# A float64 guard by absolute value and maximum, and a feed-forward half scaled by two instructions over two planes

## The chip, the core and the metric

The kernel runs on one core of a Trainium2 chip. The metric is the time of one execution on the device in microseconds (us). Five engines work side by side, each through its own queue in the order of the program: TensorE (PE, with its weight loads PEld), VectorE (DVE), ScalarE (ACT), GpSimd (POOL) and SyncE (SP), which only issues DMAs. They wait for one another through semaphores.

## The reference

Three stages follow one another: attention with a decay (4 batches, 8 heads, 576 positions, head width 64), a feed-forward network over the 2304 tokens of width 512, and a mixture of eight experts of which each token takes one. What matters here is the middle stage:

```python
h = x @ w_in                                   # x: 2304 x 512, w_in: 512 x 2048
g = np.where(h >= 1, h, np.where(h <= -1, 0.0, (h + 1) ** 2 / 4.0))
x = (g @ w_out).astype(np.float32)             # w_out: 2048 x 512
...
w_in = np.random.randn(d_model, d_ff).astype(np.float32) * (1.0 / np.sqrt(d_model))    # float64
w_out = np.random.randn(d_ff, d_model).astype(np.float32) * (1.0 / np.sqrt(d_ff))      # float64
```

The factor is a NumPy float64 scalar, and so the two weights come as float64, eight bytes an element, and the kernel turns them into float32 itself. They are read as pairs of 32-bit words: the high word holds the sign, the exponent and the upper bits of the mantissa.

## The kernel before

**Order.** A planner in the kernel (class `Order`) runs all stages as Python generators. Each `yield dve(...)`, `act(...)`, `pool2(...)`, `dma(...)` or `Use("PE", ...)` asks for an engine for so many planned nanoseconds with a priority (a smaller number goes first), and the step after it is asked for when the planned time and a latency are over. The order in which requests are granted is the order of each engine's queue; the chip then runs the queues with the real durations. A changed planned duration therefore moves instructions everywhere. `dve(n, fn, prio, fast)` plans 144 + 1.05 n ns, or 144 + 0.6 n with `fast`.

**Attention** (lines 505 to 735) takes pairs of heads: scores (line 505, tile SR), softmax on DVE, ACT and POOL (583 to 593), transposes (607), weighted sums (650, 669, 726). Raw inputs come by SP's DMAs (373), are transposed and split into a high and a low part, and are laid out in tiles `stk`, four parts each, by DMAs from `stk` to `stk` (438 to 449). The last of these for a tile, line 438, is a copy asked for at low priority.

**The feed-forward network** is done in two halves of the hidden width. `half0` (names with p) takes nine blocks of 256 tokens: block n makes hidden units in pairs (line 910, tile `hp`, two banks), `ffn_hidden` works each out (ACT 922, DVE 926 and 927, ACT 931, POOL 932), and line 1038 adds each into `accp`, a tile of four planes of 256 columns in two PSUM banks, of which there is one buffer. When all eight pieces of a block are added, `ffn_finish0` scales the four planes by 4 into a tile `x2_0` (lines 1064 on ACT and 1065 on DVE) and gives the buffer back; only then can block n + 1 add its first piece. Most of `half0` is fitted into attention; the last blocks run alone. `half1` (names with r) follows with 512 tokens at a time, then the experts (names with m). `half1` first loads its input (SP, line 891, tiles `rx`), and splits it (ACT 895, DVE 896), asked for when the last hidden unit of `half0` has been issued.

**The weights** are turned by `float64_piece`, 16 pieces of 128x512 for each half: the first 16 (tiles `wa`, raw words `war`, work tile `wax`) during attention, the other 16 (`wb`, `wbr`, `wbx`) during the last blocks of `half0`. A piece is a chain over one work tile: ACT squares the high words (853), DVE zeroes those whose square is under a bound (854), shifts and masks (856), brings back sign and top exponent bit (858), adds bits of the low word (860), ACT rounds to the high part (864), POOL subtracts for the low part (865). The work tile has one buffer, so that the next piece starts when POOL is done.

Of the kernel before, what the change touches and what calls it, by code (L numbers as in the profile page):

```python
# [13 lines left out]
AF = mybir.ActivationFunctionType  # L14
ALU = mybir.AluOpType
# [6 lines left out]
MIN64 = 2.0 ** -15 * 1.125  # L22


def f32(ap):
    return ap.bitcast(F32)
# [49 lines left out]
class Order:  # L76
# [90 lines left out]
    def done(self, ev):  # L167
        ev.n -= 1
        if ev.n == 0:
            for g in ev.waiters:  # L170
                self.at(self.now, lambda g=g: self.step(g, None))
            ev.waiters = []
# [18 lines left out]
def dve(n, fn, prio=5.0, fast=False):  # L191
    return Use("DVE", 144 + n * (0.6 if fast else 1.05), fn, prio)


def act(n, fn, prio=5.0, more=0.0):
    return Use("ACT", 155 + n / 1.2 + more, fn, prio)
# [6 lines left out]
def pool2(n, fn, prio=5.0):  # L203
    return Use("POOL", 180 + 2.3 * n, fn, prio)
# [19 lines left out]
def kernel(  # L224
# [14 lines left out]
    nc = tc.nc  # L239
    B, H, S, D = q.shape  # L240
    NT, DM = out.shape
# [5 lines left out]
    TB = 256  # L247
# [22 lines left out]
    late = {}  # L270
# [570 lines left out]
    def float64_piece(g, src, hi, lo, ok, name, prio):  # L841
        def put():
            r = fp.tile([P, DM], I64, tag="wraw", name=name + "r", bufs=2)
            nc.sync.dma_start(r.rearrange("p (c f) -> p c f", c=src.shape[1]), src)
            return r
        r = yield dma(P * DM * 8, put, 3)
        gx = yield (wx_b, 1)
        w = r.bitcast(I32).rearrange("p (n w) -> p n w", w=2)
        lw, hw = w[:, :, 0], w[:, :, 1]


        x = fp.tile([P, DM], I32, tag="wx", name=name + "x", bufs=1)
        yield act(DM, lambda: nc.scalar.activation(f32(x), f32(hw), AF.Square), prio)
        yield dve(DM, lambda: nc.vector.scalar_tensor_tensor(
            f32(hw), f32(x), MIN64 * MIN64, f32(hw), ALU.is_ge, ALU.mult), prio)
        yield dve(DM, lambda: nc.vector.tensor_scalar(
            x, hw, 3, 0x3FFFFFFF, ALU.logical_shift_left, ALU.bitwise_and), prio, True)
        yield dve(DM, lambda: nc.vector.scalar_tensor_tensor(
            x, hw, -0x40000000, x, ALU.bitwise_and, ALU.bitwise_or), prio)
        yield dve(DM, lambda: nc.vector.scalar_tensor_tensor(  # L860
            x, lw, 29, x, ALU.logical_shift_right, ALU.bitwise_or), prio)
        give(wr_b, g)
        xv = f32(x).rearrange("p (c f) -> p c f", c=src.shape[1])
        yield act(DM, lambda: nc.scalar.copy(hi, xv), prio)
        yield pool2(DM, lambda: nc.gpsimd.tensor_tensor(lo, xv, f32(hi), ALU.subtract), prio)
        give(wx_b, gx)
        done(ok)
# [78 lines left out]
    class Layer:  # L946
# [51 lines left out]
        def run2(self):  # L998
            for n in self.blocks:
                W, w = self.weights(), self.widths[n]  # L1000
                ga = yield (acc_b, 1)
                acc = None
                for u in self.units[n]:
                    yield self.g_ok[n, u]
                    GH, GL, gg = self.G.pop((n, u))
                    for k, s in enumerate(u):
                        yield W.ok[1][s]
                        if acc is None:
                            acc = psf.tile([P, 4, TB], F32, tag="acc", name=f"acc{self.name}{n}",
                                           bufs=1)  # L1010
                            if self is half0:
                                acc = [acc[:, d] for d in range(KC)]
                            else:
                                acc = [a[:, d] for a in (
                                    acc.rearrange("p (a d) t -> p a (d t)", a=2),
                                    late["psg"].tile([P, 2, 2 * TB], F32, tag="accB",
                                                     name=f"accB{self.name}{n}")) for d in range(2)]
                        gh, gl = (g[:, w * k:w * k + w] for g in (GH, GL))
                        yield Use("PE", mm(w, 3 * KC),
                                  lambda: self.second(acc, s, W, gh, gl), self.prio + 0.5,  # L1020
                                  after=0.0 if s < NF - 1 else None)
                    give(g_b, gg)
                yield from self.finish(n, acc)
                give(acc_b, ga)
            done(self.all_done)
# [34 lines left out]
    def ffn_finish0(n, acc):  # L1060
        g = yield (x2_b, 1)
        r = block("x2", g, f"x2_0_{n}")
        for d in (0, 2):
            yield act(TB, lambda: nc.scalar.mul(r[:, d], acc[d], 4.0), 0)
            yield dve(TB, lambda: nc.vector.tensor_scalar(r[:, d + 1], acc[d + 1], 4.0, None,  # L1065
                                                          ALU.mult), 0)
        go(keep(x2p[n], r, x2p_ok[n], g))

# [574 lines left out]
```

## Time and profile before

| | us |
|---|---|
| median of 3 runs (lowest, highest) | 919.18 (918.75, 919.71) |
| the profiled execution, its own time | 919.89 |
| its span, first to last instruction | 918.1 |
| TensorE busy in the span | 881.1 (96%) |
| VectorE busy | 519.9 (57%) |
| ScalarE busy | 408.7 (45%) |
| GpSimd busy | 328.5 (36%) |

Busy shares are means over stages. What counts for the time is where TensorE stands idle, for what it waits there, and the clock that it is granted (1.00 is full speed).

### The profile page before, as it was taken

How to read it: one execution, taken by the hardware profiler on the slowest of the kernel's cores; microseconds unless marked ns; L12 is line 12 of the kernel's file. 1: busy time of each engine (PE TensorE's matmuls, PEld its weight loads, DVE VectorE, ACT ScalarE, POOL GpSimd, SP SyncE). 2: the span in 40 equal slices, each digit the busy share in tenths (PEclk: the TensorE clock that was granted, in tenths of full speed). 3: DMA queues.
4: the chain of work that ended last, by engine and by line, in shares of the span. 5: the costliest groups of instructions: out<-in, count | busy, mean ns of one | idle time of the engine just before them, and what ended most of it. 6: DMA issues, size and time to landing. Idle time of an engine off the chain costs nothing. (4 is left out here: it accounts for less than half of the span.)

```text
span 918.1 us, 15151 instructions
## 1 busy us (share of the span) xinstructions
PE 881.1 (96%) x5224; PEld 752.6 (82%) x5224; DVE 519.9 (57%) x1323; ACT 408.7 (45%) x931; POOL 328.5 (36%) x342
## 2 busy tenths in 40 slices
PE   8999889999999999999799999999999999999995
PEld 6456668989998999999788888888998888888884
DVE  4878588678788747677763454376543512122331
ACT  3668677677777745443443243323333212111220
POOL 4567578565566624344342123222210132000000
PEclk9999899999999999999899999999999999999998
DMA  6669888676776407333421134744330203403220
GB/s 131 144 139 216 183 188 164 143 142 146 169 149 127 107 27 143 119 121 104 161 92 46 58 122 120 225 165 140 124 127 24 91 2 100 175 24 115 69 92 24
DMA packets 156165, 109.23 MB, mean 119 GB/s; under 512 B 103652, under 2 KB 126692, under 8 KB 156080
## 3 DMA queue, kind: packets, MB, share of 16 engines
q1 hardware_dynamic: 153080, 104.04, 43.4%
q0 software_dynamic: 3008, 4.22, 1.8%
q8 instruction: 42, 0.69, 0.3%
q14 instruction: 35, 0.29, 0.1%
HBM read 67.23 MB, written 24.75 MB: 100 GB/s over the span
## 5 line engine op out<-in xcount | busy, mean ns | idle before, releaser
L593 POOL TENSOR_SCALAR P<-P,st 128x512 f32<-128x512 f32 (+2 forms) x144 | 96.4, 676 | 108.9 <-DVE st L592 49.4
L932 POOL TENSOR_TENSOR glr<-gr,ghr 128x512 fp32r<-128x512 f32 x36 | 47.6, 1321 | 146.0 <-PE accBr L1038 100.0
L587 ACT ACTIVATE P<-P,st 128x512 f32<-128x512 f32 (+2 forms) x144 | 84.1, 585 | 34.1 <-DVE st L583 30.7
L505 PE MATMUL SR<-stk 128*128 128x256 f32 (+5 forms) x356 | 85.2, 351 | 7.7 <-DVE st L583 4.4
L910 PE MATMUL hr<-rx,wb 128*128 128x512 f32 (+1 forms) x384 | 89.0, 365 | 0.0
L1038 PE MATMUL accp<-ghp,wa 128*128 128x256 f32 x576 | 83.9, 289 | 5.2 <-DVE x L1065 5.2
L910 PE MATMUL hm<-mx,wm 128*128 128x512 f32 (+1 forms) x336 | 87.7, 381 | 0.0
L941 DVE SCALAR_TENSOR_TENSOR glm<-hm,ghm 128x512 fp32r<-128x512 f32 x36 | 24.8, 690 | 100.3 <-PE accBm L1046 75.9
L940 ACT ACTIVATE ghm<-hm 128x512 fp32r<-128x512 f32 x36 | 21.5, 598 | 132.5 <-PE accBm L1046 119.5
L1038 PEld LDWEIGHTS accp<-ghp,wa 128*128 128x128 f32 x576 | 75.5, 194 | 6.1 <-DVE x L1065 5.8
L910 PEld LDWEIGHTS hr<-rx,wb 128*128 128x128 f32 x384 | 65.7, 189 | 12.1
L583 DVE CUSTOM_DVE_ANT_0 P<-SR,masks 128x512 f32<-128x512 f32 (+1 forms) x112 | 53.6, 485 | 36.5 <-PE SR L505 30.4
L505 PEld LDWEIGHTS SR<-stk 128*128 128x128 f32 (+1 forms) x356 | 53.4, 183 | 24.6 <-issue 8.4
L932 POOL TENSOR_TENSOR glp<-gp,ghp 128x512 fp32r<-128x512 f32 x36 | 49.0, 1361 | 64.7 <-ACT ghp L931 46.8
L910 PEld LDWEIGHTS hm<-mx,wm 128*128 128x128 f32 x336 | 60.7, 188 | 12.6 <-DVE glm L941 0.3
L607 PE MATMUL T<-ident,P 128*128 128x128 f32 x384 | 64.0, 279 | 4.0 <-POOL P L593 3.0
L922 ACT ACTIVATE tr<-hr,quarter 128x512 f32<-128x512 f32 x36 | 24.7, 687 | 65.6 <-DVE gr L927 49.4
L607 PEld LDWEIGHTS T<-ident,P 128*128 128x128 f32 x384 | 43.7, 141 | 11.3 <-POOL P L593 6.7
L926 DVE SCALAR_TENSOR_TENSOR gr<-tr 128x512 f32<-128x512 f32 x36 | 24.8, 689 | 44.2 <-POOL glr L932 42.6
L1046 PE MATMUL accm<-wm,ghm 128*128 128x512 f32 x160 | 49.0, 395 | 0.0
L1038 PE MATMUL accr<-ghr,wb 128*128 128x512 f32 (+1 forms) x160 | 47.1, 376 | 0.0
L1466 POOL DMA_INDIRECT table<-ent,posi x18 | 17.8, 991 | 80.5 <-DVE ent L1455 52.0
(308 smaller groups left out, 2034.0 us busy)
## 6 DMA issues: line engine op xcount, KB each, us to landing
stk<-stk SPq DMA_DIRECT2D x26, 288.0 KB
stk<-stk SPq DMA_DIRECT2D x13, 432.0 KB
rawq<-in_q_dram SPq DMA_DIRECT2D x64, 72.0 KB
rawk<-in_k_dram SPq DMA_DIRECT2D x64, 72.0 KB
xs<-xT SPq DMA_DIRECT2D x16, 288.0 KB
x2p<-x SPq DMA_DIRECT2D x9, 512.0 KB
x2n<-nat SPq DMA_DIRECT2D x18, 256.0 KB
out_dram<-o SPq DMA_DIRECT2D x9, 512.0 KB
```

The costliest lines, as they stand in the source:

```text
L505: nc.tensor.matmul(out, a, b, start=(n == 0), stop=(n == 1), skip_group_check=skip)
L583: yield dve(w + 80, lambda: nc.vector.tensor_tensor_reduce(out=pv_, in0=so, in1=m, scale=-0.125, scalar=3e38, op0=ALU.add, op1=ALU.min, ac ...
L587: yield act(w, lambda: nc.scalar.activation(pw, pw, AF.Exp, bias=st[:, 0:1], scale=-1.0, accum_out=st[:, 1:2]), 1, 330)
L593: yield pool1(w, lambda: nc.gpsimd.tensor_scalar(pw, pw, st[:, 3:4], 1.0, ALU.mult, ALU.mult), 0)
L607: nc.tensor.transpose(T[:, P * n:P * n + P], p[:, P * kb:P * kb + P], ident)
L910: nc.tensor.matmul(oo, a[:, c, cs], x[c], start=(ip == 0 and c == 0), stop=(ip == 2 and c == KC - 1))
L922: yield act(n, lambda: nc.scalar.activation(t, oo, AF.Relu, bias=quarter, scale=0.25), 2, 60)
L926: yield dve(n, lambda: nc.vector.scalar_tensor_tensor(g, t, 0.5, t, ALU.min, ALU.mult), 2)
L932: yield pool2(n, lambda: nc.gpsimd.tensor_tensor(gl, g, f32(gh), ALU.subtract), 1)
L941: yield dve(n, lambda: nc.vector.scalar_tensor_tensor(gl, oo, 0.0, f32(gh), ALU.max, ALU.subtract), 2)
L1038: nc.tensor.matmul(acc[d][:, :w], b[:, fc, P * d:P * d + P], g, start=(fc == 0 and ip == 0 and (not narrow or d % 2 == 0)), stop=(fc == NF ...
L1046: nc.tensor.matmul(acc[a], g[:, P * a:P * a + P], b[:, fc], start=(fc == 0 and ip == 0), stop=(fc == NF - 1 and ip == 2))
```

## The change

Two edits. In `float64_piece` the guard against small magnitudes is done in another way: ACT takes the absolute value of the high words instead of the square, and DVE takes the maximum of it and the bound, in place in the work tile and with the `fast` planned duration, where it compared and multiplied into the raw tile. The shift after it reads the work tile instead of the raw one. In `ffn_finish0` four scalings of one plane each become two of two planes each: ACT takes planes 0 and 1, DVE planes 2 and 3. Lines behind the inserted one move down by one, so that 1064 and 1065 of before are 1065 and 1066 after.

```diff
         x = fp.tile([P, DM], I32, tag="wx", name=name + "x", bufs=1)
-        yield act(DM, lambda: nc.scalar.activation(f32(x), f32(hw), AF.Square), prio)
-        yield dve(DM, lambda: nc.vector.scalar_tensor_tensor(
-            f32(hw), f32(x), MIN64 * MIN64, f32(hw), ALU.is_ge, ALU.mult), prio)
+        yield act(DM, lambda: nc.scalar.activation(f32(x), f32(hw), AF.Abs), prio)
+        yield dve(DM, lambda: nc.vector.tensor_scalar(f32(x), f32(x), MIN64, None, ALU.max), prio,
+                  True)
         yield dve(DM, lambda: nc.vector.tensor_scalar(
-            x, hw, 3, 0x3FFFFFFF, ALU.logical_shift_left, ALU.bitwise_and), prio, True)
+            x, x, 3, 0x3FFFFFFF, ALU.logical_shift_left, ALU.bitwise_and), prio, True)
...
                             if self is half0:
+                                late["acc0"] = acc
                                 acc = [acc[:, d] for d in range(KC)]
...
-        for d in (0, 2):
-            yield act(TB, lambda: nc.scalar.mul(r[:, d], acc[d], 4.0), 0)
-            yield dve(TB, lambda: nc.vector.tensor_scalar(r[:, d + 1], acc[d + 1], 4.0, None,
+        acc = late["acc0"]
+        yield act(2 * TB, lambda: nc.scalar.mul(r[:, 0:2], acc[:, 0:2], 4.0), 0)
+        yield dve(2 * TB, lambda: nc.vector.tensor_scalar(r[:, 2:4], acc[:, 2:4], 4.0, None,
                                                           ALU.mult), 0)
```

The planner's order moves on all engines. Three places follow. The first is VectorE's queue where block 7 of `half0` is scaled (`x2_0_7` from `accp7`); `wbx` and `wbr` are the weight piece under work, `gp8_2` and `gp8_4` hidden units of block 8. Before:

```order
L927 SCALAR_TENSOR_TENSOR gp8_2_5723<-tp8_2_5674,gp8_2_5723 128x512 [waits DVE_49]
L854 SCALAR_TENSOR_TENSOR wbr_5656<-wbx_5761,wbr_5656 128x512 [waits DMAHW2_49,Activation_49]
L1065 TENSOR_SCALAR x2_0_7_5764<-accp7_5526 128x256 [waits DMAHW4_49,Activation_49]
L856 TENSOR_SCALAR wbx_5761<-wbr_5656 128x512 [waits DVE_49,Pool_49]
L858 SCALAR_TENSOR_TENSOR wbx_5761<-wbr_5656,wbx_5761 128x512 [waits DVE_49]
L1065 TENSOR_SCALAR x2_0_7_5764<-accp7_5526 128x256 [waits Activation_49]
L926 SCALAR_TENSOR_TENSOR gp8_4_5782<-tp8_4_5742 128x512 [waits Pool_49]
```

After:

```order
L927 SCALAR_TENSOR_TENSOR gp8_2_5702<-tp8_2_5664,gp8_2_5702 128x512 [waits DVE_49]
L854 TENSOR_SCALAR wbx_5732<-wbx_5732 128x512 [waits Activation_49]
L856 TENSOR_SCALAR wbx_5732<-wbx_5732 128x512 [waits DVE_49]
L858 SCALAR_TENSOR_TENSOR wbx_5732<-wbr_5617,wbx_5732 128x512 [waits DMAHW2_49,DVE_49]
L1066 TENSOR_SCALAR x2_0_7_5748<-accp7_5514 128x512 [waits DMAHW3_49,Activation_49]
L860 SCALAR_TENSOR_TENSOR wbx_5732<-wbr_5617,wbx_5732 128x512 [waits DVE_49]
L926 SCALAR_TENSOR_TENSOR gp8_4_5776<-tp8_4_5718 128x512 [waits Pool_49]
```

The second scaling still stands behind lines 854, 856 and 858 of one weight piece, and the scaling on VectorE still waits for a semaphore of ScalarE. On ScalarE line 853 of that piece stands just ahead of the scaling in both orders.

The second place is TensorE's queue at the end of block 7: from the last piece added to `accp7` to the first of `accp8`. Before, nothing lies between:

```order
L1038 MATMUL accp7_5526<-ghp7_6_5637,wa10_90 128x256 x4
L1038 MATMUL accp7_5526<-ghp7_6_5637,wa11_91 128x256 x4
L1038 MATMUL accp7_5526<-glp7_6_5638,wa10_90 128x256 x4
L1038 MATMUL accp8_5784<-ghp8_0_5704,wa10_90 128x256 x4
L1038 MATMUL accp8_5784<-ghp8_0_5704,wa11_91 128x256 x4
```

After, 12 matmuls of the last hidden unit lie between:

```order
L1039 MATMUL accp7_5514<-ghp7_6_5612,wa11_91 128x256 x4
L1039 MATMUL accp7_5514<-glp7_6_5613,wa10_90 128x256 x4
L910 MATMUL hp8_6_5698<-px8h_5220,wa00_88 128x256 x8
L910 MATMUL hp8_6_5698<-px8h_5220,wa01_89 128x256 x4
L1039 MATMUL accp8_5762<-ghp8_0_5680,wa10_90 128x256 x4
```

At the end of block 3 it is the other way round: 12 matmuls of a hidden unit lay between before, and none does after. Before, six pieces of block 8 stand between its start and the first matmuls of `half1` (`hr0_0` from `rx0`) and two more behind them; after, all eight stand ahead.

On ScalarE line 853, with which a weight piece begins, stands three times between the scalings of blocks 4 and 5, and again between those of 5 and 6, before; after, it stands there four times each, one for each pair of hidden units. Up to the scaling of block 7 there are 13 in both orders.

The third place is SP's queue in attention, at the tile `stk4_0`. Before:

```order
L449 DMA stk4_0_739<-stk4_0_739 64x2x576
L526 DMA stk4_0_739<-rows_79 4x2x576
L393 DMA rawv4_961<-in_v_dram 128x4x64 x2
L395 DMA rawv4_961<-in_v_dram 64x2x64
L373 DMA rawk6_980<-in_k_dram 32x18x32 x4
L844 DMA war_1019<-in_moe_w_in_dram 128x4x128
L438 DMA stk4_0_739<-stk4_0_739 64x576
L373 DMA rawq6_1033<-in_q_dram 32x18x32 x4
```

After:

```order
L449 DMA stk4_0_730<-stk4_0_730 64x2x576
L526 DMA stk4_0_730<-rows_79 4x2x576
L844 DMA war_973<-in_moe_w_in_dram 128x4x128
L373 DMA rawk6_983<-in_k_dram 32x18x32 x4
L373 DMA rawq6_1012<-in_q_dram 32x18x32 x4
L438 DMA stk4_0_730<-stk4_0_730 64x576
```

The four loads of `rawq6` now stand ahead of the copy of line 438, and the three of `rawv4` have moved to before line 449.

## Rows read from the trace of the kernel before

**Rows 1.** Windows: length, busy us of PE, PEld, DVE, ACT, POOL; PE's clock; DMA

```profile
80.00:120.00 40.00, 33.36 (x173) 23.57 (x171) 28.51 (x101) 27.66 (x74) 25.43 (x28) 0.91 0.94 189
...
440.00:480.00 40.00, 35.13 (x206) 31.61 (x205) 31.39 (x45) 19.05 (x34) 15.90 (x11) 0.91 0.45 145
480.00:520.00 40.00, 40.00 (x175) 32.42 (x174) 15.45 (x22) 11.48 (x19) 9.05 (x7) 1.00 0.16 53
```

**Rows 2.** Waits of TensorE: for whom, us in total, times, longest us

```profile
PE accp L1038 <- DVE x L1065: 5.2, 2, 4.9
PE SR L505 <- DVE st L583: 4.4, 10, 0.7
```

**Rows 3.** Timeline, end of block 7: start us, us, engine, line, [idle before <-releaser]

```profile
441.77 1.12 PE L1038 MATMUL accp<-ghp,wa 128*128 128x256 f32 x8
...
442.73 0.64 PE L1038 MATMUL accp<-glp,wa 128*128 128x256 f32 x4
...
444.01 0.66 ACT L853 ACTIVATE wbx<-wbr 128x512 f32<-128x512 f32 x1 [0.39 <-POOL wb L865]
444.58 0.37 ACT L1064 ACTIVATE x<-accp 128x256 f32<-128x256 f32 x1
...
445.65 1.48 DVE L856 TENSOR_SCALAR wbx<-wbr 128x512 int32<-128x512 int32 x1
...
447.77 0.42 DVE L1065 TENSOR_SCALAR x<-accp 128x256 f32<-128x256 f32 x1
...
448.24 2.07 PE L1038 MATMUL accp<-ghp,wa 128*128 128x256 f32 x8 [4.87 <-DVE x L1065]
...
453.38 0.42 DVE L856 TENSOR_SCALAR wbx<-wbr 128x512 int32<-128x512 int32 x1
```

**Rows 4.** Windows behind that wait, and one in attention

```profile
448.00:450.00 2.00, 1.76 (x8) 1.76 (x9) 1.99 (x4) 0.58 (x1) 0.00 (x0) 0.50 1.04 399
...
452.00:454.00 2.00, 2.00 (x18) 2.00 (x17) 1.80 (x5) 1.90 (x5) 0.50 (x1) 0.91 0.81 273
...
100.00:110.00 10.00, 9.50 (x41) 7.12 (x41) 4.74 (x19) 4.67 (x13) 4.33 (x5) 0.66 0.88 207
```

**Rows 5.** Timeline: input of `half1`, from its first DMA to its first matmuls

```profile
441.94 1.85 SPq L891 DMA_DIRECT2D rx<-xs  x4
...
458.78 2.90 PE L910 MATMUL hr<-rx,wb 128*128 128x512 f32 x12
```

**Rows 6.** Lines by form: count | busy us, mean ns | idle us before <-releaser

```profile
L854 DVE SCALAR_TENSOR_TENSOR war<-wax,war 128x512 f32<-128x512 f32 x16 | 13.3, 830 | 4.5 <-ACT wax L853 4.5
L854 DVE SCALAR_TENSOR_TENSOR wbr<-wbx,wbr 128x512 f32<-128x512 f32 x16 | 12.9, 806 | 19.5 <-ACT wbx L853 19.5
L856 DVE TENSOR_SCALAR wbx<-wbr 128x512 int32<-128x512 int32 x16 | 12.7, 794 | 0.9
...
L856 DVE TENSOR_SCALAR wax<-war 128x512 int32<-128x512 int32 x16 | 10.3, 641 | 0.6
...
L1065 DVE TENSOR_SCALAR x<-accp 128x256 f32<-128x256 f32 x18 | 7.5, 419 | 8.6 <-ACT x L1064 8.4
...
L1105 DVE SCALAR_TENSOR_TENSOR r<-accr,r 128x512 f32<-128x512 f32 x8 | 5.2, 686 | 8.2 <-PE accr L1038 8.2
```

**Rows 7.** Lines by form, ScalarE

```profile
L657 ACT COPY xT<-X 128x512 f32<-128x512 f32 x7 | 4.1, 582 | 3.4 <-PE X L650 3.4
```

**Rows 8.** Timeline of TensorE at the end of block 3

```profile
347.35 1.22 PE L1038 MATMUL accp<-ghp,wa 128*128 128x256 f32 x8 [0.37 <-DVE x L1065]
```

**Rows 9.** Timeline of POOL: its first and last instruction for `wb`, of 16

```profile
358.43 1.49 POOL L865 TENSOR_TENSOR wb<-wbx,wb 128x512 fp32r<-128x512 f32 x1 [0.74 <-ACT wb L864]
...
475.57 1.29 POOL L865 TENSOR_TENSOR wb<-wbx,wb 128x512 fp32r<-128x512 f32 x1 [4.15 <-ACT wb L864]
```

**Rows 10.** Timeline in attention: SP's last copy for `stk4_0`, TensorE behind it

```profile
94.43 0.51 SPq L438 DMA_DIRECT2D stk<-stk  x1
...
99.86 0.88 PE L505 MATMUL SR<-stk 68*64 68x288 f32 x5 [2.40 <-DMA stk<-stk]
```

## The prediction

> **What bounds the kernel now.** I read the windows first. TensorE is busy 40.00 of 40 us from 480 us on [rows 1]; the seven windows behind that one read the same up to 800 us. There its queue alone sets the pace, so a saving before 480 us moves everything behind it forward one for one, and a saving on another engine after 480 us is worth nothing. Before 480 us TensorE stands idle above all from 80 to 120 us (6.64 us) and from 440 to 480 (4.87) [rows 1]. The chain that ended last is no help: it names only the final stores.
>
> Next I read for whom TensorE waited. The longest wait is the one that `ffn_finish0` makes: 5.2 us in two waits, of which one of 4.9 [rows 2]. Its other big partner is the softmax on VectorE in attention, 4.4 us in ten small waits [rows 2].
>
> Then the timeline of that long wait [rows 3]. The last matmuls into `accp` of block 7 start at 442.73 and last 0.64, so they end at 443.37 (called T7 here). ScalarE's first scaling starts at 444.58, because line 853 of a weight piece stands ahead of it and itself waited 0.39 us for POOL. The scalings alternate between the engines, and the fourth starts only at 447.77, since 856 of that piece, ahead of it on VectorE, took 1.48 us. TensorE resumes at 448.24. The idle time is also paid a second time: the clock granted behind it is 0.50, the lower of the two levels (1.2 GHz), and the window from 452 us still has a mean of 0.91 [rows 4]. If 0.91 is a mix of 0.5 and 1.0, the clock was back at 452.36 us, so TensorE ran some 4.1 us at half speed and lost 2.05. That end costs 4.87 + 2.05 = 6.9 us in all, the dearest event in the trace.
>
> **The change, part by part.** A piece of 12 matmuls of 256 columns costs 1.44 us: eight start 0.96 us before the next four [rows 3], or 0.12 each. Those numbers do not change, so the total of TensorE's real work stays.
>
> *Scaling, block 7.* Before, the four scalings form a chain, each waiting for the other engine: 2 x 0.37 + 2 x 0.42 = 1.58 us at least [rows 3]. After, ScalarE's one scaling of 512 columns should cost about 0.58 (a PSUM copy of that form) [rows 7] and VectorE's 0.69 (a PSUM form of 512) [rows 6]. The order shows VectorE's still waiting for ScalarE. I take that as a chain of 0.58 + 0.69 + hand-overs of 0.1 = 1.4 us; if the two ran abreast it would be 0.7. So the bare chain gains only 0.2, or 0.9.
>
> What counts is what stands ahead. By the order, 853, 854, 856 and 858 of one weight piece still stand ahead of VectorE's scaling, and 853 ahead of ScalarE's. I keep 853's lateness: it ended at 444.67, T7 + 1.3. Then 854 and 856 at 0.42 each, as 856 has it undisturbed at 453.38 [rows 3], and 858 at 0.69, the form with two tensors [rows 6], give T7 + 2.8, and the scaling ends at T7 + 3.5. If 856 is held up as in the row (1.48, so 1.06 more) it is T7 + 4.6; if the weight piece is early, T7 + 0.2 + 1.4 = T7 + 1.6, where 0.2 is the least that ScalarE can follow a matmul's end by (my allowance). TensorE now has a hidden piece between, 1.44 us of cover. So it waits 2.1 us, with bounds of 0.2 and 3.2.
>
> A wait of 2.1 may or may not cost the clock: 2.40 us idle in attention was followed by a mean clock of 0.66 over 10 us [rows 4, 10]. I take half of the 2.05 us: 1.0.
>
> Behind it comes the input of `half1`. From its first DMA to its first matmuls took 458.78 - 441.94 = 16.8 us [rows 5]. That input waits in the same queues, behind the same weight pieces. After, TensorE has 1.44 + 8 x 1.44 = 13.0 us of work from T7 to those matmuls, with the wait 15.1. If the input is as late as before, counted from T7 (458.78 - 443.37 = 15.4), it costs 0.3; bounds 0 and 2, by how many conversions fall ahead. So the end of block 7 costs 2.1 + 1.0 + 0.3 = 3.4 us in place of 6.9: **-3.5**, bounds from -6.7 (0.2 alone) to +0.3 (3.2 + 2.05 + 2).
>
> *Scaling, block 3.* Its cover is gone. Before, with 1.44 us of hidden work between, TensorE waited 0.37 [rows 8]. After, it waits for the whole of 0.2 + 1.4 = 1.6: **+1.2**. If the two scalings run abreast, 0.9 and +0.5; if something stands ahead, I allow 1.3 more. At the other ends of blocks the order leaves hidden units or attention work between, at least 2.8 us, so I cost those at nothing; they would cost up to 1.6 each without it.
>
> The Trainium skill, "PSUM — Partial Sum Buffer", section "PSUM bank collisions raise a hardware error", says that two engines may not access one bank at once and that different banks run clean. By that rule the new halves, which lie in two banks, could run abreast, and the sum would gain 0.7 more at block 3. The waits in the order speak against it here; no row of before shows it.
>
> *The guard.* 32 instructions of line 854 change from a form with two tensors (mean 830 and 806 ns) to one like line 856 (641 and 794 ns) [rows 6]. ScalarE's Abs I cost like Square; table loads are six in both orders. The bounds per instruction: from 0.69 to 0.42, as just said, if nothing disturbs it, or no saving. By the means VectorE saves 16 x 0.19 + 16 x 0.01 = 3.2 us, at most 32 x 0.27 = 8.6. It lies beside TensorE's work except where TensorE waits for VectorE. Those waits are 4.4 us in attention [rows 2], and of the 3.2 us 3.0 are freed there; VectorE is busy 28.5 us in 40 at its densest [rows 1], so most of the freed time falls into gaps. I choose a fifth of the waits: **-0.8**, bounds 0 and -4.4.
>
> The rule that speaks against this part is in the Trainium skill, "SBUF — State Buffer", section "Who interferes with whom": an exclusive lock on ports that VectorE shares with GpSimd, taken by simple one-tensor forms in their fast mode as much as by those with two tensors. By it the new form is held up as often as the old. The row of 856 at 1.48 us where its mean is far less [rows 3, 6] agrees. It would make this part 0, a rival below.
>
> *Attention's order.* At `stk4_0` the low-priority copy of line 438 now stands behind four loads of `rawq6` more, and three of `rawv4` fewer. TensorE already waited 2.40 us for that copy, issued at 94.43 and waited for until 99.86 [rows 10]. The loads moved ahead of line 449 may fall where SP waits anyway, so the copy goes out between 0 and some 2 us later (four issues at 0.51, that of line 438 [rows 10]). Everything else in attention is reshuffled too, with the same work. I take **+0.8**, bounds -2.4 (that wait gone) and +4 (2 late, and as much again at the lower clock).
>
> *Weight pieces and hidden units.* Four pieces in place of three share the queues with the hidden units of two blocks; up to block 7 there are 13 either way, each lighter on VectorE, so I cost this at nothing. It is the slower rival.
>
> **Sum.** -3.5 + 1.2 - 0.8 + 0.8 = -2.3 us against the profiled execution's 919.89, which is 917.6. That execution was 0.71 over the median of 919.18, so I forecast 916.9.
>
> **The rivals.**
> - *Bigger gain.* The weight pieces finish early, so that block 7's scaling meets free queues (0.2 us of wait, no loss of clock), and attention's waits on VectorE shrink by half (-2.2): -6.7 + 1.2 - 2.2 + 0.8 = -6.9, or 912.3. For it: VectorE's load falls. Against: 853 still stands ahead, and waited for POOL, which the change does not speed up. I place this case around 913.5.
> - *No gain, since the change doesn't do what it says.* The maximum is held up by POOL as often as the old guard (0 by the row of 856 at 794 beside 806), and the scaling still ends at T7 + 4.6, so that 3.2 us and the whole clock loss stay: 3.2 + 2.05 + 0.3 - 6.9 = -1.3; with +1.2 and +0.8 it is +0.7. Time 919.9.
> - *Slower.* In blocks 5 and 6 each pair of hidden units now has a weight piece in its queues. A pair is four pieces of TensorE's work, 5.76 us. Weight pieces came every 7.81 us before (475.57 - 358.43 over 15) [rows 9], part of it because they were ordered so. With eight in step, a piece that takes longer than 5.76 us holds up the hidden units queued behind it. At 6.3 us it is 8 x 0.54 = 4.3 us, or 921.2; from there on it decides. For it: the hold-ups of 856 [rows 3] stay. Against: each pair has the other bank of `hp` as slack, and the same 13 pieces fitted before block 7.
>
> **How the numbers follow.** About 0.2% (1.84 us) is what a measurement of this kernel tells from no change; the bounds are 917.3 and 921.0. Forecast: 0.45, own range 915 to 919, of which 0.28 below 917.3. Bigger gain: 0.22, all faster. No gain: 0.16, all within. Slower: 0.17, of which 0.15 above 921.0 and 0.02 within. That is 0.50 faster, 0.35 within, 0.15 slower. The range of 8 in 10 reaches to the bigger gain and into the slower case: 912.3 to 921.5.
>
> **What would show it.** Line 854 at a mean near 0.64 to 0.80; the scalings at about 0.58 and 0.69, nine on each engine, VectorE's starting after ScalarE's ends; a wait of some 1.6 us on `accp` at the end of block 3 and 2 us at block 7 in place of 4.87; the first matmuls of `half1` 15 to 16 us after the last piece of block 7; idle time of TensorE before 130 us within 2 us of now. I am wrong if block 7 still waits 4 us or more, if a wait for `stk` passes 4 us, or if waits on ScalarE's 922 or 931 appear in blocks 5 and 6.

## The result, and the profile after

The changed kernel takes 910.82 us (median of 4 runs, 909.01 to 912.46) against 919.19 of the kernel before beside it: a ratio of 0.9892, 95% interval 0.987 to 0.9914. The forecast was 916.9. The direction was right; the gain is 8.4 us where 2.3 were forecast, and the time lies outside the range. Its profiled execution took 909.01 us with a span of 907.4, which is 10.7 less than before. It is the fastest of its four.

The lines by form (count, busy us, mean ns, idle before), answering to [rows 6]:

```profile
L858 DVE SCALAR_TENSOR_TENSOR wbx<-wbr,wbx 128x512 int32<-128x512 int32 x16 | 17.7, 1107 | 0.3
...
L854 DVE TENSOR_SCALAR wax<-wax 128x512 f32<-128x512 f32 x16 | 8.9, 554 | 3.9 <-ACT wax L853 3.9
L856 DVE TENSOR_SCALAR wax<-wax 128x512 int32<-128x512 int32 x16 | 8.7, 545 | 0.1
L854 DVE TENSOR_SCALAR wbx<-wbx 128x512 f32<-128x512 f32 x16 | 8.5, 534 | 20.7 <-ACT wbx L853 20.7
...
L856 DVE TENSOR_SCALAR wbx<-wbx 128x512 int32<-128x512 int32 x16 | 6.8, 426 | 0.5
L1066 DVE TENSOR_SCALAR x<-accp 128x512 f32<-128x512 f32 x9 | 6.1, 683 | 3.2 <-ACT x L1065 3.1
L1065 ACT ACTIVATE x<-accp 128x512 f32<-128x512 f32 x9 | 5.3, 591 | 4.2 <-PE accp L1039 4.1
```

Line 854 fell from 830 and 806 ns to 554 and 534, below the forecast of 641 to 794; 856 behind it on `wbx`, whose input the edit moves into the work tile, fell from 794 to 426, while 858 rose from 879 to 1107. The scalings have the forecast lengths, and VectorE's waits for ScalarE's, 3.1 us over nine.

TensorE's waits (us, times, longest), answering to [rows 2]:

```profile
PE accp L1039 <- DVE x L1066: 4.1, 5, 1.6
PE T L607 <- POOL P L593: 3.7, 5, 1.0
PE SR L505 <- DVE st L583: 2.9, 5, 1.1
PE hp L910 <- ACT tp L922: 2.7, 3, 1.8
...
PE SR L505 <- DMA stk<-stk: 1.5, 1, 1.5
```

The windows (as in [rows 1, 4]), with two shorter ones that are used further down:

```profile
28.00:34.00 6.00, 4.71 (x25) 3.04 (x26) 5.01 (x15) 3.33 (x10) 2.78 (x4) 1.00 0.96 203
80.00:120.00 40.00, 32.95 (x193) 24.34 (x191) 29.66 (x104) 29.44 (x78) 27.05 (x31) 1.00 0.98 205
92.00:104.00 12.00, 9.50 (x53) 6.59 (x52) 5.92 (x26) 7.78 (x23) 6.97 (x8) 1.00 0.97 190
100.00:110.00 10.00, 9.38 (x62) 8.19 (x63) 7.29 (x24) 6.31 (x18) 5.29 (x6) 1.00 0.89 226
120.00:320.00 200.00, 198.60 (x1493) 185.20 (x1493) 160.49 (x540) 148.61 (x375) 124.81 (x140) 1.00 0.65 145
440.00:480.00 40.00, 39.48 (x213) 33.89 (x212) 25.40 (x37) 17.57 (x31) 15.23 (x11) 1.00 0.31 101
```

TensorE is idle as long as before from 80 to 120 us (7.05 against 6.64), but the clock, 0.66 from 100 to 110 us on [rows 4], is 1.00. From 120 to 320 us its idle time is 1.40 us. The same window of the kernel before shows 5.74:

```profile
120.00:320.00 200.00, 194.26 (x1439) 178.58 (x1440) 158.37 (x539) 148.19 (x375) 127.09 (x140) 1.00 0.68 149
```

The timeline at the end of block 7, answering to [rows 3, 5]:

```profile
435.05 0.64 PE L1039 MATMUL accp<-glp,wa 128*128 128x256 f32 x4
...
435.74 0.67 ACT L853 ACTIVATE wbx<-wbr 128x512 f32<-128x512 f32 x1 [0.38 <-POOL wb L865]
436.31 0.58 ACT L1065 ACTIVATE x<-accp 128x512 f32<-128x512 f32 x1
436.44 0.43 DVE L854 TENSOR_SCALAR wbx<-wbx 128x512 f32<-128x512 f32 x1 [1.88 <-ACT wbx L853]
...
437.97 0.68 DVE L1066 TENSOR_SCALAR x<-accp 128x512 f32<-128x512 f32 x1
...
438.71 1.23 PE L1039 MATMUL accp<-ghp,wa 128*128 128x256 f32 x8 [1.60 <-DVE x L1066]
...
449.35 0.74 PE L1039 MATMUL accp<-glp,wa 128*128 128x256 f32 x4 [0.43 <-POOL glp L932]
...
451.37 0.85 PE L910 MATMUL hr<-rx,wb 128*128 128x512 f32 x3
```

853, 854, 856 and 858 stand ahead of the scaling as before, but pass in 2.3 us. TensorE waits 1.60 us in place of 4.87 and keeps its clock.

Three points of TensorE's queue have the same work ahead of them in both orders (but for two warming matmuls): the first piece of block 4, that of block 8, and the first matmul into `accr` of `half1`. They divide the gain:

| start, us | before | after | gained up to it | gained since the point above |
|---|---|---|---|---|
| first piece of block 4 | 347.35 | 340.68 | 6.67 | 6.67 |
| first piece of block 8 | 448.24 | 438.71 | 9.53 | 2.86 |
| first into `accr` | 472.58 | 462.26 | 10.32 | 0.79 |

### The profile page after: what moved, and what is told of

It is laid out like the page before. It is cut to its first block, busy times and chain, and to the rows that moved or that the text cites. A ratio compares the mean times of both kernels' runs of the same rounds, so it can differ in the third digit from the quotient of the medians.

```text
span 907.4 us, 15092 instructions
## 1 busy us (share of the span) xinstructions
PE 875.9 (97%) x5228; PEld 750.5 (83%) x5228; DVE 511.7 (56%) x1314; ACT 406.9 (45%) x922; POOL 325.6 (36%) x342
## 4 chain that ended last, share of the span: by engine, by line
PE 81%; DVE 8%; DMA 3%; ACT 3%; POOL 2%; issue 2%; SPq 0%; POOLq 0%; DVEq 0%; ACTq 0%
PE hm L910 11%; PE hr L910 11%; PE hp L910 8%; PE accp L1039 6%; PE accm L1047 6%; PE SR L505 6%; PE accr L1039 6%; PE accBr L1039 6%; PE accBm L1047 5%; PE T L607 4%; PE X L650 2%; PE X L669 2%; PE U L726 2%; PE lps L1513 2%; PE gt L1219 1%
## 5 line engine op out<-in xcount | busy, mean ns | idle before, releaser
L593 POOL TENSOR_SCALAR P<-P,st 128x512 f32<-128x512 f32 (+2 forms) x144 | 94.2, 661 | 106.6 <-DVE st L592 55.5
L505 PE MATMUL SR<-stk 128*128 128x256 f32 (+5 forms) x356 | 83.2, 349 | 4.6 <-DVE st L583 2.9
L505 PEld LDWEIGHTS SR<-stk 128*128 128x128 f32 (+1 forms) x356 | 52.4, 181 | 20.2 <-issue 10.3
L1039 PE MATMUL accp<-glp,wa 128*128 128x256 f32 x288 | 46.4, 284 | 0.4 <-POOL glp L932 0.4
```

The source lines that it names most:

```text
L505: nc.tensor.matmul(out, a, b, start=(n == 0), stop=(n == 1), skip_group_check=skip)
L593: yield pool1(w, lambda: nc.gpsimd.tensor_scalar(pw, pw, st[:, 3:4], 1.0, ALU.mult, ALU.mult), 0)
L1039: nc.tensor.matmul(acc[d][:, :w], b[:, fc, P * d:P * d + P], g, start=(fc == 0 and ip == 0 and (not narrow or d % 2 == 0)), stop=(fc == NF ...
```

## The experiments

Each kernel was timed against the kernel before in the same set; a ratio has its 95% interval behind it.

### Each edit alone

`guard_alone` has the first part of the diff, `scaling_alone` the second.

> Only the guard's edit, with its planned cost; the four scalings stay. The changed kernel's trace gains 7.7 us up to block 4 of half0 (340.68 in place of 347.35, with 1.0 us more of wait at block 3) and 3.65 behind it. Order theory (the new planned cost reshuffles attention into a better order): 912 to 914 us, and the same as with the old guard under the new plan. Duration theory (VectorE's shorter instruction relieves attention): also 912 to 915, but the same as with the new guard under the old plan. If the scalings made the gain: 918 to 920.

Measured: 914.0 us, 0.9943 (0.9927 to 0.9959).

> Only the scaling's edit; the guard stays. TensorE's order is that of before up to the first scaling at about 199 us, so the lower clock at 100 us and the waits ahead of it should stay. Both theories on the guard: the end of block 7 is some 3 us cheaper, 915 to 917.5 us. If the scalings made the gain in attention too: 911 to 913.

Measured: 919.91 us, 0.9995 (0.9984 to 1.0006). So the edit that I gave the gain makes none by itself, and the one that I costed at -0.8 us makes nearly 6. The scaling does what was forecast, and more: in the trace of `scaling_alone` the wait at the end of block 7 is 1.54 us and block 8 starts at 443.16, 5.1 us earlier than before. It is given back inside block 8. The timeline there (start, us, engine, line, idle before and its releaser):

```profile
452.42 0.68 DVE L896 TENSOR_TENSOR rx<-rx 128x512 fp32r<-128x512 f32 x1
...
453.00 4.83 POOL L932 TENSOR_TENSOR glp<-gp,ghp 128x512 fp32r<-128x512 f32 x1 [3.80 <-ACT ghp L931]
...
456.03 0.68 DVE L896 TENSOR_TENSOR rx<-rx 128x512 fp32r<-128x512 f32 x1
...
457.31 1.07 DVE L896 TENSOR_TENSOR rx<-rx 128x512 fp32r<-128x512 f32 x1 [0.60 <-ACT rx L895]
...
457.88 1.23 PE L1039 MATMUL accp<-glp,wa 128*128 128x256 f32 x4 [3.75 <-POOL glp L932]
```

POOL's subtraction for the last hidden unit takes 4.83 us; the median of its 36 is 1.29. From 449.67 us to 456.71 VectorE goes from one instruction to the next without a pause, most of them with two tensors (896, 926, 927, 854, 858, 860), and POOL ends 1.1 us after the first pause. The Trainium skill, "SBUF — State Buffer", section "Who interferes with whom", says that a two-input VectorE instruction contends with a GpSimd instruction that reads SBUF, through a port pair that is locked. The row agrees, and adds that a whole run of such instructions passes before the subtraction ends. That the run is what holds POOL is read from the traces: in the changed kernel VectorE pauses for 0.60 us at 448.16, and the same subtraction, begun at 447.79, takes 1.51 us. No experiment broke up the run itself.

### Duration or order

`guard_old_plan` plans the new guard at the old cost, so that TensorE's and SP's queues stay as before; `old_guard_new_plan` plans the old guard at the new cost.

```diff
 guard_old_plan: on the guard edit
-        yield dve(DM, lambda: nc.vector.tensor_scalar(f32(x), f32(x), MIN64, None, ALU.max), prio, True)
+        yield dve(DM, lambda: nc.vector.tensor_scalar(f32(x), f32(x), MIN64, None, ALU.max), prio)
 old_guard_new_plan: on the kernel before
-            f32(hw), f32(x), MIN64 * MIN64, f32(hw), ALU.is_ge, ALU.mult), prio)
+            f32(hw), f32(x), MIN64 * MIN64, f32(hw), ALU.is_ge, ALU.mult), prio, True)
```

> The new guard's instructions, planned at the old cost: TensorE's and SP's queues read as before, row for row, and VectorE's too but for the changed forms. Order theory: 918 to 920 us, no change. Duration theory: 912 to 915.

Measured: 913.68 us, 0.9939 (0.9926 to 0.9951).

> The old guard's instructions, planned at the new guard's cost, with four scalings: the queues of the run with the guard alone, with the old forms. Order theory: within 1 us of the guard alone, 912 to 914.5. Duration theory: 918 to 921.

Measured: 920.08 us, 1.0017 (0.9994 to 1.0039). For the guard by itself it is the shorter instruction that pays; the order that the planner makes for it is worth nothing. In the trace of `guard_old_plan` the copy of `stk` is waited for a little less than on [rows 10]:

```profile
99.23 0.88 PE L505 MATMUL SR<-stk 68*64 68x288 f32 x5 [1.97 <-DMA stk<-stk]
```

and behind it the clock is kept, where [rows 4] has 0.66:

```profile
100.00:110.00 10.00, 9.00 (x58) 7.43 (x57) 7.03 (x25) 7.28 (x20) 5.78 (x7) 1.00 0.93 232
```

### Half of the pieces, and the edits crossed

Two kernels have the new guard in one half of the pieces only, in the order of before: `guard_first_16` in `wa` (attention), `guard_second_16` in `wb` (last blocks). `both_old_plan` is the changed kernel with the guard planned at the old cost, `new_order_old_guard` the changed kernel with the old guard planned at the new cost. The edits are those of the last diff, under `if name.startswith("wa")` or `"wb"`.

> The kernel before with the new guard only in the first 16 weight pieces (wa, turned during attention), planned at the old cost, so that the rows of TensorE and SyncE stay as before. Theory (two separate savings, one in attention with the clock at 100 us, one in the last blocks): the stretch up to the first piece of block 4 shortens by some 4 us as it did with the guard in all 32, and nothing behind it, so about 915 to 916 us (0.9955). Rival A (all of the 6 us hang on attention, the rest being only moved forward into a better alignment): 913.5 (0.994). Rival B (the saving is made by the second 16 pieces): 919 (1.000).

Measured: 918.41 us, 0.9982 (0.9969 to 0.9995).

> The kernel before with the new guard only in the second 16 weight pieces (wb, turned beside the last blocks), planned at the old cost; rows of TensorE and SyncE as before. Theory: attention stays as before, with the wait of about 2.4 us for the copy of stk and the lower clock behind it; the wait at the end of block 7 falls from 4.9 to about 3.8, so about 917 to 918 us (0.998). Rival A: 919 (1.000). Rival B: 913.5 (0.994).

Measured: 917.55 us, 0.9969 (0.9955 to 0.9983). Both halves pay, but the first less than I expected. Its trace waits 2.65 us for `stk` and has the clock of before behind it:

```profile
100.67 1.46 PE L505 MATMUL SR<-stk 68*64 68x288 f32 x5 [2.65 <-DMA stk<-stk]
...
100.00:110.00 10.00, 9.00 (x36) 6.80 (x37) 3.94 (x17) 4.23 (x12) 3.82 (x6) 0.66 1.00 221
```

It also has a clock of 0.72 from 44 to 50 us. Up to there its instructions are those of `guard_old_plan`, whose trace is at 1.00 from 20 us on. The first piece of block 4 starts at 346.55 here and at 343.22 there (347.35 before), so some 3 of the 6 us of `guard_old_plan` go with the clock in attention. Why one kernel keeps it and the other doesn't is not shown. Chance from one execution to the next does not look like the whole of it: the five executions of `guard_old_plan` lie between 913.55 and 914.10 us, the twelve of `guard_first_16`, in a later set, between 916.71 and 919.75.

> The changed kernel with the new guard planned at the old cost: the new instructions of both edits in the order of the scaling edit alone. Theory (durations, not the order that the new guard was planned into): as the changed kernel, 909 to 912.5 us (0.9895 to 0.9925), with the stall of the scaling edit alone on the last hidden unit of block 8 (3.75 us) mostly gone, since the weight pieces ahead of it are lighter. Rival (the two edits need the new order to add up): about 914 us (0.994), as the guard alone, with that stall still over 2 us.

Measured: 917.1 us, 0.9961 (0.9945 to 0.9977): the rival. The wait of 3.75 us on `glp` is there as in `scaling_alone`, behind a subtraction of 4.83 us again. The lighter guard doesn't remove that stall.

> The changed kernel with the old guard's instructions in its place, planned at the new cost: the order of the changed kernel row for row, the scalings as changed, only the duration of line 854 as before. Theory: 918 to 920 us (0.9985 to 1.001), with line 854 at a mean near 0.8 us. Rival (the order of both edits together brings the part beyond the sum of the single edits): about 916.5 us (0.997).

Measured: 919.38 us, 0.9992 (0.9981 to 1.0004). The whole order with the old guard is worth nothing either. So new instructions in the order of the scaling alone give -2.9 us and the order without them -0.6; together they gave -8.4, and -8.9 in a later set. The two need each other.

### The hold-up of POOL, taken away

In `both_old_plan` the one slow subtraction is given to VectorE, planned as before:

```diff
+        eng = nc.vector if nm == "p8_6" else nc.gpsimd
-        yield pool2(n, lambda: nc.gpsimd.tensor_tensor(gl, g, f32(gh), ALU.subtract), 1)
+        yield pool2(n, lambda: eng.tensor_tensor(gl, g, f32(gh), ALU.subtract), 1)
```

> The kernel of both_old_plan with one instruction moved: the low part of the last hidden unit of block 8 (line 931 there, POOL, 4.83 us in its profile where others take 1.3 to 1.9) is subtracted on VectorE, at its place in the program. Theory (GpSimd gets no turn while VectorE runs 8 instructions of two tensors back to back): the wait of 3.75 us for it falls under 1 us and the clock behind it stays at 1.00, so about 4 to 5 us less than both_old_plan, 912 to 913 (0.9925), and with it the scaling edit pays without the new order. Rival (that wait comes from the input chain, not from POOL's stretch): TensorE waits as long at the same place or at the first matmuls of the second half, 916 to 917 (0.9965).

Measured: 911.35 us, 0.9896 (0.9874 to 0.9917), 5.7 us less than `both_old_plan` (0.9961). The timeline and the clock of `both_old_plan` at that place:

```profile
455.60 1.23 PE L1038 MATMUL accp<-glp,wa 128*128 128x256 f32 x4 [3.75 <-POOL glp L931]
...
456.00:460.00 4.00, 4.00 (x12) 3.26 (x12) 1.64 (x4) 0.67 (x1) 1.22 (x1) 0.51 0.22 78
```

and the timeline with the subtraction on VectorE:

```profile
449.95 1.22 PE L1039 MATMUL accp<-ghp,wa 128*128 128x256 f32 x8 [0.52 <-ACT ghp L930]
450.65 0.68 DVE L932 TENSOR_TENSOR glp<-gp,ghp 128x512 fp32r<-128x512 f32 x1
451.38 0.73 PE L1039 MATMUL accp<-glp,wa 128*128 128x256 f32 x4 [0.22 <-DVE glp L932]
```

That shows where the gain of the scaling went: a new wait of 3.75 us with a clock of 0.51 behind it. The saving is made there and not in attention: from the first piece of block 8 to the first into `accr` the two kernels, in the same order, take 26.6 us (441.20 to 467.82) and 21.1 (440.53 to 461.61). One instruction on another engine reaches what the new order of the changed kernel reaches: there most of the input splits (896) stand behind the subtraction.

### The changed kernel again, and by halves of its guard

> The changed kernel unaltered, once more, beside the three other kernels of this set. Theory (its gain beyond the guard's is that its order meets neither of two stalls with a lowered clock behind it, at 100 us and in the last block): 909 to 912.5 us (0.989 to 0.992), runs with the lower clock at 100 us near 912.3 and those without near 909.3. Rival (the result on record depended on the chip that it ran on): near 916 us (0.996).

Measured: 911.6 us (909.11 to 919.16, 12 runs), 0.9916 (0.9893 to 0.9939). The gain stands, but one kernel spreads over 10 us. Its profiled execution has a span of 910.8, and of the 3.4 us over the first 3.2 are there at block 4 (343.86 against 340.68). Its windows, beside the same two of the first execution above:

```profile
28.00:34.00 6.00, 4.61 (x21) 3.73 (x22) 3.70 (x13) 3.09 (x9) 2.69 (x5) 0.72 1.00 208
92.00:104.00 12.00, 11.70 (x43) 7.83 (x42) 5.08 (x22) 7.05 (x20) 7.74 (x9) 0.58 1.03 186
```

The same program with the same small waits ahead (1.04 us on POOL and 0.66 on ScalarE at 87 to 92 us in both traces) keeps the full clock in one execution and falls to 0.50 in the other.

The same order row for row, with the new guard in the first or the second 16 pieces:

> The changed kernel's order row for row, with the new guard only in the first 16 weight pieces and the old guard's instructions in the other 16. Theory (in this order each half of the guard saves by itself: the first some 6 us of waits in attention, the second the wait at the end of block 7 with its clock): between the two whole kernels, about 913 to 915 us (0.993), a first piece of block 4 near 341 us and a wait of 3 us or more at the end of block 7 with a clock of 0.50 behind it. Rival (all of it is made in the last blocks): 918 to 920 (0.999). Rival (all in attention): 909 to 912 (0.990).

Measured: 916.79 us, 0.9962 (0.9946 to 0.9978).

> The changed kernel's order, with the old guard in the first 16 weight pieces and the new one in the other 16. Theory: first piece of block 4 near 346.7 us as with the old guard in all, a wait of about 1.6 us at the end of block 7 without loss of clock, about 913 to 915 us (0.993). Rival (all in the last blocks): 909 to 912. Rival (all in attention): 918 to 920.

Measured: 914.91 us, 0.995 (0.993 to 0.997). Each half saves by itself: against the -0.6 us of `new_order_old_guard` the first gives -3.3 and the second -5.2 more. That adds up to -9.1, near the -8.4 and -8.9 of the changed kernel. Of the end of block 7 the second decides: with the old guard there (`new_order_old_guard`)

```profile
448.79 2.07 PE L1039 MATMUL accp<-ghp,wa 128*128 128x256 f32 x8 [3.40 <-DVE x L1066]
```

and with the new one in `wb` alone

```profile
443.68 1.21 PE L1045 MATMUL accp<-ghp,wa 128*128 128x256 f32 x8 [1.60 <-DVE x L1072]
```

The lengths say the rest: the first eight matmuls take 2.07 us at half the clock, 1.21 at the full one. From block 4 to `accr` `new_order_old_guard` takes 474.61 - 346.74 = 127.9 us, `after_order_second_16` 467.24 - 345.68 = 121.6, and the changed kernel 121.6 too.

### The clock's price: waits filled with matmuls

TensorE got extra matmuls of 128x128, whose results nobody reads, ahead of an instruction that waits, so that it works while it would wait. They leave the computation as it is.

```diff
 in the scores that wait for stk (before_filled_wait, after_filled_wait)
+                for _ in range(12 if i == 4 else 0):
+                    nc.tensor.matmul(bank[:, 0, :P], ident, ident, start=True, stop=True, skip_group_check=True)
 ahead of block 8 (before_filled_block8: 30, before_filled_block8_short: 21)
+                                nc.tensor.matmul(D[:, 0, :P], ident, ident, start=True, stop=True, skip_group_check=True)
 ahead of two transposes (after_filled_88: 7 and 4, after_filled_88_short: 4 and 2)
+                    nc.tensor.matmul(T[:, :P], ident, ident, start=True, stop=True)
```

> The kernel before with 12 extra matmuls of 128x128 on TensorE, whose results are overwritten, ahead of the scores that wait for the late copy of stk at 97 us; at 0.14 us each they take 1.7 of the 2.4 us in which TensorE waits. All rows of the other engines stay. Theory (of that wait's price some 3.4 us are the lower clock behind it): the copy lands as before, the clock stays at 1.00 in 100 to 110 us, and the time falls by 3 to 3.5 us, to about 916 (0.9965). Rival (the lower clock costs nothing there since TensorE then waits for others anyway): 919 to 920 (1.000).

Measured: 917.79 us, 0.9971 (0.9958 to 0.9984): 2.7 us, a little under the 3 to 3.5 expected, for a clock of 1.00 from 100 to 110 us in the trace.

> The kernel before with 30 extra matmuls of 128x128 into an unused bank of PSUM, 4.2 us at 0.14 each, in the wait of 4.87 us between the last piece of block 7 and the first of block 8. Theory (2.05 us of that end's price are the lower clock): the idle time shrinks to about 0.7 us, the clock stays at 1.00 in 444 to 456 us, and the time falls by 2 us, to about 918 (0.998). Rival (TensorE then only waits for the next hidden unit or the input of the second half): 920 (1.000).

Measured: 920.12 us, 0.9996 (0.9982 to 1.0009), inconclusive: an extra matmul is two records of 0.11 us, and the 30 took 6.6 us where the wait is 4.87. From the first piece of block 8 to `hr` it took 8.72 us in place of 10.54, so the clock gave 1.8 and the overrun took it. With 21:

> The kernel before with 21 extra matmuls in the wait between blocks 7 and 8 (4.6 us at 0.22 each, where 30 took 6.6 and overran the wait of 4.87). Theory: no loss by the fillers now and the 1.8 to 2 us of the lower clock saved, 918.5 (0.998). Rival: 920.5 (1.000).

Measured: 919.29 us, 0.9983 (0.997 to 0.9996), with the full clock behind it:

```profile
448.00:452.00 4.00, 4.00 (x35) 4.00 (x35) 2.52 (x5) 2.90 (x5) 1.29 (x1) 1.00 1.03 355
```

From the first piece of block 8 to `hr` it took 8.73 us, 1.8 less than before, so the 2.05 us that the forecast put on the clock there was about right; of the whole time 1.3 us came off.

> The changed kernel with the same 12 extra matmuls at the same place, where its profile has a wait of 1.51 us. Theory: nothing where the clock was kept, -3 us in executions that lost it, so a median near 909.5 and a narrower spread, 909 to 910 (0.989). Rival (the clock plays no part there): as the changed kernel, 909 to 912.5, or 0.2 us more.

Measured: 915.02 us, 0.9933 (0.9909 to 0.9957): a miss, slower than the changed kernel by 3.4. In its trace the clock fell at 90 us already, TensorE came late to the wait for `stk`, there was nothing left to fill, and the 12 matmuls were pure cost.

> The changed kernel with 7 and 4 extra matmuls of 128x128 ahead of the two transposes that wait at 87 and 88.8 us (1.04 and 0.66 us), written into the tiles that the transposes then overwrite. Theory (the executions near 912 us and above lose the clock behind these waits): the clock stays at 1.00 in 84 to 100 us and the runs gather at 909 to 910 (0.988 to 0.990). Rival (the clock falls for another reason, or later in attention instead): as the changed kernel, 909 to 914 with a median near 911.6, or more by the extra matmuls.

Measured: 912.7 us, 0.9914 (0.9896 to 0.9932), with fillers that were too long.

> The changed kernel with 4 and 2 extra matmuls (0.9 and 0.4 us, under the waits of 1.04 and 0.66). Theory: the clock stays at 1.00 in 84 to 100 us in nearly all executions, so 909 to 911 us with few above 912 (0.989). Rival: spread and median as the changed kernel, 911.6 (0.9905).

Measured: 911.4 us (910.34 to 912.76, 5 runs), 0.9901 (0.9888 to 0.9915). The clock stays at 1.00 from 80 to 112 us in the trace, and the median is that of the changed kernel. Whether the spread is smaller can't be told: these five lie within 2.4 us, the four of the first set within 3.5. Its profiled execution lost the clock at 30 to 38 us instead (0.67 and 0.90), where nothing was filled. No version here beats the changed kernel by more than the spread.

## Why the prediction was wrong, step by step

**End of block 7, -3.5: right in size, in part by luck.** Block 4 to `accr` shortened by 2.86 + 0.79 = 3.65 us. The wait was 1.60 for 2.1. 854 and 856 took 0.43 each for the 0.42 that I chose, and VectorE's scaling ended at 438.65, T7 + 2.96 with T7 = 435.69, for T7 + 3.5. I charged half of the clock loss and none came. The first matmuls of `half1` started 15.7 us behind T7, within the 15 to 16 forecast. But the cause was half missed: `scaling_alone` and `new_order_old_guard` show that the scaling needs both the lighter pieces of `wb` and the later input splits. With the scaling, the new order and the old guard, block 4 to `accr` takes 127.9 us, 2.6 more than before (125.2). The new guard in `wb` takes 6.3 off that: 4.0 up to the first piece of block 8, and 2.3 behind it, where the clock no longer falls.

**Block 3, +1.2: right.** The wait there is 1.41 us in place of the 0.37 of [rows 8], and the scalings do not run abreast:

```profile
339.31 0.60 ACT L1065 ACTIVATE x<-accp 128x512 f32<-128x512 f32 x1 [2.34 <-PE accp L1039]
339.94 0.69 DVE L1066 TENSOR_SCALAR x<-accp 128x512 f32<-128x512 f32 x1 [2.25 <-ACT x L1065]
340.68 1.22 PE L1039 MATMUL accp<-ghp,wa 128*128 128x256 f32 x8 [1.41 <-DVE x L1066]
```

ScalarE followed the end of the last matmul (339.27) by 0.04 us, where I had allowed 0.2.

**The guard, -0.8 with bounds 0 and -4.4: mis-sized; this is the step that failed.** By the queue of before it measured -6.0 (`guard_old_plan`), and 4.1 of that are there at block 4 in its trace; in the order of the changed kernel its half in `wa` alone gives -3.3. It went wrong in three ways.

The price per instruction was set by the old 856. The new 854 came out at 554 and 534 ns, and its 32 instructions together are 8.8 us shorter (26.2 before by [rows 6], 17.4 after) for the 3.2 that the means gave and the 8.6 that I allowed at most. Line 856 is 7.5 us shorter in all (23.0 and 15.5), but 3.3 of that come with the new order alone (19.7 in `new_order_old_guard`), and 858 took back 3.5.

Only TensorE's waits on VectorE were counted, though the guard is a link of a chain to ScalarE and POOL. With equal queues (`new_order_old_guard` and after) TensorE's waits on VectorE's `st` fell from 4.5 to 2.9 us, and those on POOL's `P` from 5.8 to 3.7.

And the guard's term had nothing for the clock in attention, though [rows 4] showed its loss at 100 us, which `before_filled_wait` prices at 2.7 us. In the trace that kept the clock the guard in the order of before was worth 4.1 us up to block 4 (`guard_old_plan`), in the one that lost it 0.8 (`guard_first_16`).

**Attention's order, +0.8: wrong sign.** The copy of `stk` was waited for 1.51 us, less than before. For the whole kernel the order by itself is worth nothing that can be told (1.0017 in `old_guard_new_plan`, 0.9992 in `new_order_old_guard`), but in the second that is a sum of two parts: its trace loses 2.6 us from block 4 to `accr`, as said above, and gains before that. In the two traces with the order of the changed kernel and the old guard in `wa` the first piece of block 4 starts at 346.74 and 345.68 (`after_order_second_16`), 0.6 and 1.7 us earlier than before in spite of the longer wait at block 3, and the clock from 100 to 110 us is 1.00. Whether order and guard help each other in attention the traces do not decide. TensorE's idle time from 120 to 320 us is 5.74 us before, 3.93 with the guard alone (`guard_old_plan`), 4.26 with the order alone (`new_order_old_guard`), and with both 1.40, 2.24 (`after_again`) and 3.46 (`after_order_first_16`).

Together attention up to block 4 gained 6.67 + 1.04 = 7.7 us in the profiled execution, where my two terms cancelled. With the end of block 7 and block 3 that is -3.65 + 1.04 - 7.7 = -10.3 of the span's -10.7. That execution is the fastest of its four; in the profiled one of `after_again`, which lost the clock twice in attention, the 7.7 are 4.5.

**The rivals.** "Bigger gain" came nearest, by another way than it named: attention, not a block 7 without any wait. "No gain" fell with line 854's mean: against the 0.43 and 0.68 us that the new and the old form take undisturbed the means are 0.10 to 0.12 and 0.13 to 0.15 us longer, so both are held up, and the new one stays the shorter. Of "slower" there is a trace: waits on line 922 in block 6 (1.77 us and two of 0.49, 2.7 in all against 1.8 before). The rule by which the halves would run abreast can't be judged here: in the program VectorE's scaling waits for ScalarE's as the order shows, and two tiles for one accumulator were not tried.

What stays open is the division of attention's gain between clock and waits, and between order and guard, in the median of the changed kernel: its executions lose the clock at different places, and only single ones were profiled.

## What to carry to other kernels

Cost an edit on a chain by the chain's length and by what stands behind it on every engine, not by the waits on the engine that is edited. Where a profile shows the lower clock behind a wait, put the clock into the term of whatever moves that wait, and look at more than one profiled execution before trusting where it fell. When an edit frees a stall and the time stays, look for the next stall within the same stage: here one instruction that was four times its usual length.

## What the runs showed of the hardware that I had not expected

A POOL subtraction of 1.29 us lasted 4.83 while VectorE ran its queue without a pause, in both kernels with that order; moving the one instruction to VectorE, where it took 0.68, gave 5.7 us.

TensorE's clock falls to 0.50 in some executions and not in others at the same place of the same program. In the 12 runs of `after_again` the time goes from 909.11 to 919.16 us. Of the changed kernel's two profiled executions, one keeps the full clock from 20 to 120 us, the other loses it at 30 to 34 and at 90 to 104 us and comes 3.2 us later to block 4. No long wait is needed for it: the idle stretches ahead were about 1 us and less.

The maximum with a constant on one 128x512 tensor takes 0.43 us undisturbed, the old compare-and-multiply of two tensors 0.68; the means are 0.53 to 0.55 in the changed kernel and 0.81 to 0.83 in the kernel before.
